# Attention scores split into high and low parts: two full passes and one shared pass for a pair of key tiles

## The chip, the core and the metric

The kernel runs on one core of a Trainium2 chip. The core has a matrix engine (TensorE, PE in the profile, with PEld for the loading of its weights), a vector engine (DVE), a scalar engine (ACT), GpSimd (POOL) and SyncE (SP); here SP does nothing but issue transfers, and POOL little else. The metric is the device time of one execution in microseconds (us). Before the change it is 1505.49 us, the median of 3 runs (1505.46 to 1505.99).

## The reference

Three stages follow each other; everything is float32.

```
scores = (1/S) * z @ z.T            # z: 2 x 3008 x 64, S = 3008
x      = u * (maximum(scores, 0)**2 @ v)      # u, v: 2 x 3008 x 256
h      = x @ moe_w_in                # 6016 x 256 by 256 x 2048
g      = (a0 + a1 h + a2 h^2 + a3 h^3) / (1 + |b0| |h| + |b1| h^2 + 1e-6)
y      = g @ moe_w_out               # back to 6016 x 256
h2     = y @ moe2_w_in;  g2 = max(h2, 0) + alpha * min(h2, 0)
out    = g2 @ moe2_w_out
```

Only the product z @ z.T is touched by the change.

## The kernel before

**Products in parts.** TensorE is fed with a rounded float32 (fp32r). So each operand is split into a high part (the rounded value) and a low part (what the rounding left), and a product is the sum of passes: high by high, high by low and low by high. A pass is one matmul of up to 512 columns with a weight load of 128 by 128 ahead of it. For the values of the attention and both dense stages a pass fills all 128 rows of the array. For the scores z has only 64 features, so high and low are stacked: a tile zA holds the high part of z in partitions 0 to 63 and the low part in 64 to 127 (`load_z`, L691 and L694), and a tile zB holds the same with the halves exchanged. With zA as weights, a pass over zA gives high by high plus low by low (L846), and a pass over zB gives the two mixed products (L847). zB is copied out of zA by two transfers of SP for each block of 512 queries (`a_begin`, L736); that of the first block is computed on ACT and DVE (L704, L707).

**Tiling.** The work of the attention goes by batch (2), block of 512 queries (6, the last with 448) and pair of key tiles (12 pairs of 2 times 128 keys). As scores are symmetric, only pairs on or right of the diagonal are computed. The others are the transposes of finished ones: DVE transposes a result (L772), SP writes it to memory (L787, "rt") and reads it back when it is due (L820, "rr"). A computed pair goes through `a_scores`: four matmuls (two key tiles, two passes each) into PSUM, relu with the scale on ACT (L853 or L861), the square (L866), and high and low for the next product (L449, L454). In the two last blocks of 448 queries the columns come in cuts of 256 and 192, so a computed pair is eight matmuls. `a_values` multiplies a pair with v: eight matmuls of L887 and four of L898.

**PSUM.** While no step of the first dense stage has begun, computed pairs take turns in several double tiles (two single tiles s, h, acc); after that all of them use the two single tiles s_78 and s_79.

**What sets the order.** Nothing is issued as it is written. Each operation is recorded in a `Plan` with a guessed duration, the buffers that it reads and writes, and the order of TensorE; a list scheduler (`Plan.order`) then runs the plan in guessed time and gives each other engine the ready operation that is due first. Constants such as PACE, SAME, SOONER, SAFE and DEBT steer it. While the attention runs, steps of the first dense stage ("m1", L1012 to L1029 on ACT and DVE) and the decoding of weights ("dec", L554 to L635) are let in whenever the vector work that is booked (`plan.debt`) is below DEBT; each matmul takes its guessed time off that debt. What has not got in by the end of the attention follows after it, among the steps of the two dense stages ("h" and "m" are their hidden tiles, "ghi" and "glo" the parts of the activations).

Of the kernel before, what the change touches and what calls it, by code (L numbers as in the profile page):

```python
# [14 lines left out]
PSUM = bass.MemoryType.PSUM  # L15
DRAM = bass.MemoryType.DRAM

PT, ZP, XP = 48, 8, 4

RING = 2048  # L20

CAREFUL = False

PACE = 25.0

SAME = 0.13

SOONER = 30.0

WIRE = 0.7  # L30

SAFE = 1.0

BACK = 3

PRE = 3

AFTER = 4.0

FIRST, NEXT = 6, 4  # L40

FILL, DEBT, EDGE = 0.97, 4.0, 4.0

LAG_A, LAG_M = 3, 2

HEAD, X1 = 38, 18

R0, RD = 2, 2.5

WARM = 13  # L50

KEEP = 2

BOUND = 122879.9921875

# [18 lines left out]
class Plan:  # L74
# [8 lines left out]
    def add(self, eng, dur, fn, r=(), w=(), level="att", after=0.0, horizon=None, data=0.0):  # L83
        o = Op()
        o.eng, o.dur, o.fn, o.level, o.after, o.data = eng, dur, fn, level, after, data
        o.horizon = horizon
        if eng == "PE":
            self.pe = o
            self.debt = max(self.debt - FILL * dur, 0.0)
        elif eng == "DVE":  # L90
            self.debt += dur
        o.pin = self.pe
        o.i = len(self.ops)
        o.next, o.need, o.allocs, o.takes, o.bufs = [], 0, [], [], []
        preds = {}

        def keys(x):
            if isinstance(x, tuple):
                return [(x[0], x[1])]
            return [(x, p) for p in range(x.parts)]  # L100

        seen = set()
        for group, writes in ((r, False), (w, True)):
            for x in group:
                b = x[0] if isinstance(x, tuple) else x
                if id(b) not in seen:
                    seen.add(id(b))
                    o.bufs.append(b)
                    b.users += 1
                    b.ops.append(o)  # L110
                for k in keys(x):
                    kk = (id(k[0]), k[1])
                    for p in self.wrote.get(kk, ()):
                        preds[p.i] = p
                    if writes:
                        for p in self.read.get(kk, ()):
                            preds[p.i] = p
                if writes and b.kind:
                    o.takes.append(b)
                    if not b.held:  # L120
                        b.held = True
                        o.allocs.append(b)
        for group, writes in ((r, False), (w, True)):
            for x in group:
                for k in keys(x):
                    kk = (id(k[0]), k[1])
                    if writes:
                        self.wrote[kk] = [o]
                        self.read[kk] = []
                    else:  # L130
                        self.read.setdefault(kk, []).append(o)
        for p in preds.values():
            p.next.append(o)
            o.need += 1
        self.ops.append(o)
        return o
# [54 lines left out]
    def order(self):  # L191
# [30 lines left out]
                queue[b.kind].append((o.late, o.i, o, b))  # L222
        head = dict.fromkeys(rooms, 0)
        for q in queue.values():
            q.sort()

        def fits(o, now):
            want = {}
# [81 lines left out]
def relu2_attention_rational_mlp_prelu_mlp(  # L310
# [56 lines left out]
    def big_room(nm):  # L367
        return room(nm, F32R, (P, 2, 2, 256))

    def z_room(nm):  # L370
        return Buf("z", lambda i: zp.tile([P, QB], F32R, tag=f"z{i}", name=nm))

    def x_room(nm):
        return Buf("x", lambda i: xp.tile([P, QB], F32R, tag=f"x{i}", name=nm), 1)
# [25 lines left out]
    def act(n, fn, r, w, psum=False, ptr=0, level="att", horizon=SOON):  # L400
        return plan.add("ACT", n / 1200 + (0.051 if psum else 0.094) + 0.094 * ptr, fn, r, w, level, horizon=horizon)

    def dve(n, fn, r, w, ptr=0, fast=False, level="att", horizon=SOON):
        return plan.add("DVE", n / (1920 if fast else 960) + 0.068 + 0.061 * ptr, fn, r, w, level, horizon=horizon)
# [252 lines left out]
        )  # L657
        store[jp] = t

    zA = {}  # L660

    zB = {}

    def q_side(z, b, j):

        t = z[b, j]().rearrange("p (s a r) -> p a s r", s=4, a=4)
        if qn[j] == QB:
            return [(0, QB, t)]
        return [(0, QB // 2, t[:, 0:2]), (QB // 2, qn[j], t[:, 2:4, 0:3])]

    def load_z(b, g):

        raw = room("zraw", F32, (P, 2 * QB))
        n = qn[g]
        sp(
            n / 2,
            lambda: nc.sync.dma_start(out=raw()[:, 0:n], in_=zt[b, :, g * QB : g * QB + n]),
            [],
            [raw],
        )  # L680
        m = n
        if n % P:
            sp(
                32,
                lambda: nc.sync.dma_start(out=raw()[:, n : n + HALF], in_=zt[b, :, S - HALF : S]),
                [],
                [raw],
            )
            m += HALF
        t = z_room("zA")  # L690
        dve(m, lambda: nc.vector.tensor_copy(t()[:, 0:m], raw()[:, 0:m]), [raw], [t], fast=True)  # L691
        dve(
            m,
            lambda: nc.vector.tensor_tensor(  # L694
                t()[HALF:P, 0:m], raw()[HALF:P, 0:m], t()[HALF:P, 0:m].bitcast(F32), ALU.subtract
            ),
            [raw, t],
            [t],
        )
        zA[b, g] = t  # L700
        if (b, g) == (0, 0):
            q = z_room("zB")
            zB[b, g] = q
            act(m, lambda: nc.scalar.copy(q()[HALF:P, 0:m], raw()[HALF:P, 0:m]), [raw], [q])  # L704
            dve(
                m,
                lambda: nc.vector.tensor_tensor(  # L707
                    q()[0:HALF, 0:m], raw()[0:HALF, 0:m], t()[0:HALF, 0:m].bitcast(F32), ALU.subtract
                ),
                [raw, t],  # L710
                [q],
            )

    blocks = [(b, j) for b in range(B) for j in range(NQ)]
# [11 lines left out]

    def a_begin(b, j):

        if (b, j) in zB:
            return  # L730
        n = qn[j]
        t, z = z_room("zB"), zA[b, j]
        for p0 in (0, HALF):
            sp(
                n / 4,
                lambda p0=p0: nc.sync.dma_start(  # L736
                    out=t()[p0 : p0 + HALF, :n].bitcast(F32),
                    in_=z()[HALF - p0 : P - p0, :n].bitcast(F32),
                ),
                [z],  # L740
                [(t, p0 // HALF)],
                horizon=SOONER,
            )
        zB[b, j] = t

    def folded(b, i, j):
        return i < j
# [65 lines left out]
    def a_scores(b, j, kp):  # L813
        n = qn[j]
        if folded(b, kp // 2, j):
            r, d = room("rr"), turned[b, kp // 2, j]
            s0 = kp % 2 * 2
            sp(
                n,
                lambda: nc.sync.dma_start(out=r()[:, :, :n], in_=d()[s0 : s0 + 2].rearrange("s p k -> p s k")),  # L820
                [d],
                [r],
            )
            ahl[b, j, kp] = hi_lo(r, n, kp)
            return
        r = room("r")

        pair = None
        if not opened:
            turn = kp % 3 if (b, j) == (0, 0) else direct[0] % 2  # L830
            direct[0] += 1
            if turn == 1:
                pair = h_room("sp")
            elif turn == 2:
                t2 = Buf("acc1", lambda i: at["acc1"][i])
                pair = t2
        for i in range(2):
            k = 2 * kp + i
            zk = zA[b, k // 4]
            s = (pair, i) if pair is not None else s_room("s")  # L840
            ks = slice((k % 4) * P, (k % 4 + 1) * P)

            def mm(s=s, i=i, zk=zk, ks=ks):
                o = pair()[:, i, :n] if pair is not None else s()[:, :n]
                for (c0, c1, x), (_, _, y) in zip(q_side(zA, b, j), q_side(zB, b, j)):
                    nc.tensor.matmul(o[:, c0:c1], zk()[:, ks], x, start=True, stop=False)  # L846
                    nc.tensor.matmul(o[:, c0:c1], zk()[:, ks], y, start=False, stop=True)  # L847

            pe(n, 2 if n == QB else 4, mm, [zk, zA[b, j], zB[b, j]], [s])
            if pair is None:  # L850
                act(
                    n,
                    lambda s=s, i=i: nc.scalar.activation(r()[:, i, :n], s()[:, :n], AF.Relu, scale=1.0 / S),  # L853
                    [s],
                    [(r, i)],
                    psum=True,
                )
        if pair is not None:
            act(
                2 * n,  # L860
                lambda: nc.scalar.activation(r()[:, :, :n], pair()[:, :, :n], AF.Relu, scale=1.0 / S),  # L861
                [pair],
                [r],
                psum=True,
            )
        act(2 * n, lambda: nc.scalar.activation(r()[:, :, :n], r()[:, :, :n], AF.Square), [r], [r])  # L866
        ahl[b, j, kp] = hi_lo(r, n, kp)
        if folded(b, j, kp // 2):
            turn_block(b, j, kp, r)
# [457 lines left out]
```

## Time and profile before

| | |
|---|---|
| median of 3 runs | 1505.49 us |
| profiled execution, its own time | 1505.41 us |
| its span | 1503.6 us |
| PE busy | 1493.3 us, 99% |
| DVE busy | 1408.5 us, 94% |
| ACT busy | 1193.4 us, 79% |
| POOL busy | 71.3 us, 5% |
| granted TensorE clock | 9 (full) in all 40 slices |

The profiled execution took 1.8 us more than its span, which runs from its first to its last recorded instruction. A record of a matmul or of a vector instruction reaches into that of the next one, since the engines work in a pipeline: the price of one in a dense row is the distance from its start to the next start, not its own length. Busy shares count the union of the records, and so make an engine look somewhat fuller than it is.

### The profile page before, as it was taken

Reading aid. Unit: us, or ns where it says so; the run is one execution under the profiler, and the core shown is the slowest. Engines: PE = TensorE matmul, PEld = TensorE weight load, DVE = VectorE, ACT = ScalarE, POOL = GpSimd, SP = SyncE. Lnnn points to the kernel's source line nnn. Section 1 sums busy time; section 2 is a strip of 40 time slices with the busy share of each in tenths; the row PEclk is TensorE's granted clock in tenths of the full one; section 3 lists DMA queues with packets and bytes.
Section 4 is the critical chain, followed back from the end, with each engine's and each line's share of the span. In section 5 each row is a group of like instructions: output and inputs, shape, how many; then the busy total and the mean of one; then the engine's idle time right before and its main releaser. Section 6 shows DMA issues by size and latency. Waiting matters only on the chain.

```text
span 1503.6 us, 17908 instructions
## 1 busy us (share of the span) xinstructions
PE 1493.3 (99%) x6677; PEld 1247.2 (83%) x6677; DVE 1408.5 (94%) x1449; ACT 1193.4 (79%) x1406; POOL 71.3 (5%) x98
## 2 busy tenths in 40 slices
PE   9999999999999999999999999999999999999999
PEld 7888888788788887888888888888888888888888
DVE  8998999989999999999999999999999999899963
ACT  8888877888987687778779778878777887788754
POOL 1000000101212110000000000000000000000000
PEclk9999999999999999999999999999999999999999
DMA  7987547576878773100000000000000000000000
GB/s 202 243 242 186 151 143 236 152 195 188 238 217 248 246 248 129 43 28 29 15 28 14 29 29 28 29 15 28 29 29 14 27 17 28 28 26 29 15 1 25
DMA packets 178887, 144.51 MB, mean 96 GB/s; under 512 B 132704, under 2 KB 147568, under 8 KB 178800
## 3 DMA queue, kind: packets, MB, share of 16 engines
q1 hardware_dynamic: 169168, 108.75, 25.8%
q0 software_dynamic: 9632, 34.62, 6.9%
q8 instruction: 52, 0.85, 0.2%
q14 instruction: 35, 0.29, 0.1%
HBM read 83.90 MB, written 56.62 MB: 93 GB/s over the span
## 4 chain that ended last, share of the span: by engine, by line
PE 90%; DVE 7%; issue 2%; DMA 1%; ACT 0%; SPq 0%; DVEq 0%; ACTq 0%
PE acc L887 35%; PE acc L898 17%; PE h L960 6%; PE h L959 6%; PE h L958 6%; PE m L959 5%; PE m L958 5%; PE m L960 5%; PE s L847 2%; PE s L846 2%; DVE alo L454 1%; PE acc L877 1%; DVE ghi L1026 1%; DVE t L1028 0%; DVE ab L1027 0%
## 5 line engine op out<-in xcount | busy, mean ns | idle before, releaser
L887 PE MATMUL acc<-ghi,w 128*128 128x512 f32 (+1 forms) x1472 | 360.7, 387 | 0.0
L887 PEld LDWEIGHTS acc<-ghi,w 128*128 128x128 f32 x1472 | 275.6, 188 | 54.9
L887 PE MATMUL acc<-ahi,vt 128*128 128x512 f32 (+1 forms) x1152 | 283.0, 387 | 2.4 <-DVE ut L931 1.5
L887 PEld LDWEIGHTS acc<-ahi,vt 128*128 128x128 f32 x1152 | 215.8, 188 | 46.8 <-DVE ut L931 1.9
L1014 ACT ACTIVATE t<-h,sc 128x1024 f32<-128x1024 f32 (+1 forms) x96 | 114.0, 1187 | 104.4 <-PE h L960 86.1
L898 PE MATMUL acc<-glo,w 128*128 128x512 f32 (+1 forms) x736 | 195.0, 387 | 0.0
L898 PEld LDWEIGHTS acc<-glo,w 128*128 128x128 f32 x736 | 137.8, 188 | 27.5
L960 PE MATMUL h<-xhi,w 128*128 128x512 f32 (+1 forms) x408 | 156.2, 383 | 0.0
L958 PE MATMUL h<-xhi,w 128*128 128x512 f32 (+1 forms) x408 | 156.1, 383 | 0.0
L959 PE MATMUL h<-xlo,w 128*128 128x512 f32 (+1 forms) x408 | 156.1, 383 | 0.0
L1081 ACT ACTIVATE m<-m,sc 128x512 f32<-128x512 f32 (+1 forms) x180 | 117.0, 693 | 43.8 <-PE m L960 41.0
L1017 DVE SCALAR_TENSOR_TENSOR ab<-sq,cb,ab 128x1024 f32<-128x1024 f32 (+1 forms) x96 | 120.7, 1258 | 29.3 <-ACT sq L1012 29.1
L898 PE MATMUL acc<-alo,vt 128*128 128x512 f32 (+1 forms) x552 | 146.6, 386 | 0.0
L958 PE MATMUL m<-xhi,w 128*128 128x512 f32 (+1 forms) x360 | 139.4, 387 | 1.6 <-DVE m L1087 1.4
L959 PE MATMUL m<-xlo,w 128*128 128x512 f32 (+1 forms) x360 | 139.3, 387 | 0.9 <-DVE xlo L454 0.9
L960 PE MATMUL m<-xhi,w 128*128 128x512 f32 (+1 forms) x360 | 139.2, 387 | 0.0
L1022 ACT ACTIVATE sq<-ab,one 128x1024 f32<-128x1024 f32 (+1 forms) x96 | 110.3, 1149 | 20.6 <-DVE t L1019 20.5
L454 DVE TENSOR_TENSOR glo<-m,ghi 128x1024 fp32r<-128x1024 f32 (+1 forms) x96 | 114.9, 1197 | 11.0 <-ACT ghi L449 11.0
L898 PEld LDWEIGHTS acc<-alo,vt 128*128 128x128 f32 x552 | 103.6, 188 | 20.3 <-DVE alo L454 0.2
L1026 DVE TENSOR_TENSOR ghi<-t,sq 128x1024 fp32r<-128x1024 f32 (+1 forms) x96 | 114.9, 1196 | 5.0 <-ACT sq L1023 4.0
L1087 DVE TENSOR_TENSOR m<-m 128x1024 f32<-128x1024 f32 (+1 forms) x90 | 108.5, 1205 | 10.1 <-ACT m L1081 10.1
L1029 DVE TENSOR_TENSOR glo<-t,sq 128x1024 fp32r<-128x1024 f32 (+1 forms) x96 | 114.9, 1197 | 2.0
(99 smaller groups left out, 2645.0 us busy)
## 6 DMA issues: line engine op xcount, KB each, us to landing
rt<-rt SPq DMA_DIRECT2D x220, 128.0 KB, 3.2
rr<-rt SPq DMA_DIRECT2D x40, 512.0 KB, 5.1
rr<-rt SPq DMA_DIRECT2D x20, 448.0 KB, 4.9
wraw<-in_moe_w_in_dram POOLq DMA_DIRECT2D x16, 512.0 KB, 5.4
wraw<-in_moe_w_out_dram POOLq DMA_DIRECT2D x16, 512.0 KB, 5.5
wd<-dec POOLq DMA_DIRECT2D x16, 512.0 KB, 5.0
w<-wd POOLq DMA_DIRECT2D x16, 512.0 KB, 6.2
x2d<-x SPq DMA_DIRECT2D x11, 512.0 KB, 2.6
```

The source lines that it names most:

```text
L454: lambda: nc.vector.tensor_tensor(lo(), src(), hi().bitcast(F32), ALU.subtract),
L887: nc.tensor.matmul(acc()[:, e, :n], w()[:, k, i, e * P : (e + 1) * P], hi()[:, i, :n], start=first and i == 0 and k == 0, stop=False,)
L898: nc.tensor.matmul(acc()[:, e, :n], w()[:, 0, i, e * P : (e + 1) * P], lo()[:, i, :n], start=False, stop=last and i == both - 1,)
L958: nc.tensor.matmul(acc, w_hi, hi, start=first, stop=False)
L959: nc.tensor.matmul(acc, w_hi, lo, start=False, stop=False)
L960: nc.tensor.matmul(acc, w_lo, hi, start=False, stop=last)
L1014: act(N, lambda: activation(c(t), c(h), AF.Identity, scale=a3, bias=a2), [h], [t], psum=True, ptr=2, **kw)
L1017: dve(N, lambda: stt(c(ab), c(sq), b1, c(ab), ALU.mult, ALU.add), [sq, ab], [ab], ptr=1, **kw)
L1022: act(N, lambda: activation(c(sq), c(ab), AF.Abs_reciprocal_sqrt, bias=one), [ab], [sq], ptr=1, **kw)
L1026: dve(N, lambda: tt(c(hi), c(t), c(sq), ALU.mult), [t, sq], [hi], **kw)
L1029: dve(N, lambda: tt(c(lo), c(t), c(sq), ALU.mult), [t, sq], [lo], **kw)
L1081: lambda i=i, f=f: nc.scalar.activation(t()[:, i, :n], h()[:, i, :n], AF.Copy, scale=al[:, f : f + 1]),
```

## The change

The tile zK replaces zA as weights. In it the halves alternate from key tile to key tile: in even key tiles partitions 0 to 63 hold the high part and 64 to 127 the low part, in odd key tiles the other way round. For the queries there are two tiles: zH with the high part in both halves, zL with the low part in both halves. One pass with zK as weights over zH gives high by high plus low by high (L859 of the changed kernel), one for each key tile. The missing high by low needs 64 rows only. For the even key tile these are the upper 64 partitions of zK, for the odd one the lower 64, so two matmuls of 64 rows in different halves of the array, into two PSUM tiles, do it for the pair (L856). The product of low by low is left out. Both small matmuls are booked in the plan as one operation of ROWS = 1.2 passes.

zH and zL of each further block are copied from zK by eight transfers of 64 partitions by two pieces of 128 columns (L745), where two transfers made zB before. Those of the first block are computed on DVE, and its zK on ACT. The first pair of all has its low matmuls last instead of first. There are 9 instead of 8 rooms for z tiles, and some of the planner's constants are other ones.

```diff
-PT, ZP, XP = 48, 8, 4
+PT, ZP, XP = 48, 9, 4
+ROWS = 1.2
-SOONER = 30.0
+SOONER = 45.0
...
     def load_z(b, g):
...
-        t = z_room("zA")
-        dve(m, lambda: nc.vector.tensor_copy(t()[:, 0:m], raw()[:, 0:m]), [raw], [t], fast=True)
-        dve(
-            m,
-            lambda: nc.vector.tensor_tensor(
-                t()[HALF:P, 0:m], raw()[HALF:P, 0:m], t()[HALF:P, 0:m].bitcast(F32), ALU.subtract
-            ),
-            [raw, t],
-            [t],
-        )
+        t = z_room("zK")
...
+            dve(m, lambda: nc.vector.tensor_copy(t()[:, 0:m], raw()[:, 0:m]), [raw], [t], fast=True)
+        for odd in range(2):
+            def low(odd=odd):
+                rows = slice(0, HALF) if odd else slice(HALF, P)
+                z = t()[rows].rearrange("p (c o k) -> p c o k", o=2, k=P)[:, :, odd]
+                r = raw()[rows, 0:m].rearrange("p (c o k) -> p c o k", o=2, k=P)[:, :, odd]
+                nc.vector.tensor_tensor(z, r, z.bitcast(F32), ALU.subtract)
+            dve(m // 2, low, [raw, t], [t])
...
     def a_begin(b, j):
...
-        for p0 in (0, HALF):
-            sp(
-                n / 4,
...
+        for store, nm in ((zH, "zH"), (zL, "zL")):
+            t = z_room(nm, 4)
+            for odd in range(2):
+                src = HALF * (odd ^ (nm == "zL"))
+                for p0 in (0, HALF):
...
+                        nc.sync.dma_start(out=cols[0][p0 : p0 + HALF], in_=cols[1][src : src + HALF])
+                    sp(64, move, [z], [(t, 2 * odd + p0 // HALF)], horizon=SOONER)
...
     def a_scores(b, j, kp):
...
-                for (c0, c1, x), (_, _, y) in zip(q_side(zA, b, j), q_side(zB, b, j)):
-                    nc.tensor.matmul(o[:, c0:c1], zk()[:, ks], x, start=True, stop=False)
-                    nc.tensor.matmul(o[:, c0:c1], zk()[:, ks], y, start=False, stop=True)
...
+        def lows(c0, c1, y):
+            for i in range(2):
+                rows = slice(HALF * i, HALF * i + HALF)
+                nc.tensor.matmul(at_i(i)[:, c0:c1], zk()[rows, keys_of(i)], y[rows], start=not late, stop=late)
+        def highs(i, c0, c1, x):
+            nc.tensor.matmul(at_i(i)[:, c0:c1], zk()[:, keys_of(i)], x, start=late, stop=not late)
...
+                pe(ROWS * z, 1, lambda: lows(c0, c1, y()), [zk, zL[b, j]], hs)
```

In the order of TensorE, a computed pair later in the attention reads thus; s_78 and s_79 are the PSUM tiles of the two key tiles, acc_81 the sum of the values. Before:

```order
L898 MATMUL acc_81<-alo,vt 128x512 x4
L846 MATMUL s_79<-zA 128x512
L847 MATMUL s_79<-zB,zA 128x512
L846 MATMUL s_78<-zA 128x512
L847 MATMUL s_78<-zB,zA 128x512
L887 MATMUL acc_81<-ahi,vt 128x512 x8
```

And now:

```order
L922 MATMUL acc_81<-alo,vt 128x512 x4
L856 MATMUL s_79<-zL,zK 128x512
L856 MATMUL s_78<-zL,zK 128x512
L859 MATMUL s_79<-zH,zK 128x512
L859 MATMUL s_78<-zH,zK 128x512
L911 MATMUL acc_81<-ahi,vt 128x512 x8
```

There are four matmul instructions still (6677 in all, as before), but the two of L856 have 64 rows each; both PSUM tiles are now written by the first two instructions, where the second tile was first touched by the third one.

On the queue of SP, at the change from the first to the second and third query block, before (rt and rr are the written and reread transposes, xd the result of a block):

```order
L820 DMA rr<-rt_0_1_99 128x2x512
L736 DMA zB<-zA 64x512 x2
L787 DMA rt_0_5_103<-rt 32x16x64 x6
L787 DMA rt_0_5_103<-rt 32x16x32 x2
L937 DMA xd_0_104<-ut 128x1024
```

And now:

```order
L946 DMA ut<-in_u_dram 128x2x512
L745 DMA zL<-zK 64x2x128
L791 DMA rt_0_5_103<-rt 32x16x64 x4
L745 DMA zH<-zK 64x2x128 x3
L791 DMA rt_0_5_103<-rt 32x16x64 x2
L791 DMA rt_0_5_103<-rt 32x16x32 x2
L745 DMA zH<-zK 64x2x128
L824 DMA rr<-rt_0_2_100 128x2x512
L745 DMA zL<-zK 64x2x128
L961 DMA xd_0_105<-ut 128x1024
```

The copies of z stand in ones and threes between the transfers of the transposes; on the whole queue they are 88 where they were 22.

On TensorE at the end of the attention, before (h_80 belongs to the first dense stage, m to the second; 18 steps of the first dense stage stand ahead of the last row of alo,vt in the whole program):

```order
L887 MATMUL acc_82<-ghi,w 128x512 x8
L898 MATMUL acc_82<-glo,w 128x512 x4
L887 MATMUL acc_81<-ahi,vt 128x448 x8
L898 MATMUL acc_81<-alo,vt 128x448 x4
L958 MATMUL m<-xhi,w 128x512
```

And now (14 steps of the first dense stage stand ahead of the last row of alo,vt):

```order
L922 MATMUL acc_81<-alo,vt 128x448 x4
L982 MATMUL h_80<-xhi,w 128x512
L983 MATMUL h_80<-xlo,w 128x512
L984 MATMUL h_80<-xhi,w 128x512
L911 MATMUL acc_82<-ghi,w 128x512 x8
L922 MATMUL acc_82<-glo,w 128x512 x4
L982 MATMUL m<-xhi,w 128x512
```

Four steps of the first dense stage have gone from the attention into what follows it. On DVE, 27 of the 32 decoded weights are begun by the last alo of the attention, where all 32 were, and 14 steps of the first dense stage instead of 17.

## Rows read from the trace of the kernel before

**Rows 1.** The page's busy times, and the granted clock in 40 slices
```profile
PE 1493.3 (99%) x6677; PEld 1247.2 (83%) x6677; DVE 1408.5 (94%) x1449; ACT 1193.4 (79%) x1406; POOL 71.3 (5%) x98
...
PEclk9999999999999999999999999999999999999999
```

**Rows 2.** The page's chain that ended last, by engine
```profile
PE 90%; DVE 7%; issue 2%; DMA 1%; ACT 0%; SPq 0%; DVEq 0%; ACTq 0%
```

**Rows 3.** Waits of PE: us in total, times, longest
```profile
PE acc L887 <- DVE ut L931: 1.5, 1, 1.5
...
PE s L847 <- DVE zB L707: 0.3, 1, 0.3
```

**Rows 4.** Timeline of PE, one computed pair: start us, length us
```profile
60.60 0.40 PE L846 MATMUL s<-zA 128*128 128x512 f32 x1
60.83 0.40 PE L847 MATMUL s<-zB,zA 128*128 128x512 f32 x1
...
61.53 0.39 PE L887 MATMUL acc<-ahi,vt 128*128 128x512 f32 x1
```

**Rows 5.** Timeline of PE, a pair in cuts of 256 and 192
```profile
226.76 0.28 PE L846 MATMUL s<-zA 128*128 128x256 f32 x1
...
227.66 0.64 PE L887 MATMUL acc<-ahi,vt 128*128 128x512 f32 x2
```

**Rows 6.** Groups of PE by form: count, busy us, mean ns
```profile
L846 PE MATMUL s<-zA 128*128 128x512 f32 x124 | 49.9, 402 | 0.1
...
L846 PE MATMUL h<-zA 128*128 128x512 f32 x28 | 11.5, 412 | 0.0
...
L846 PE MATMUL acc<-zA 128*128 128x512 f32 x8 | 3.6, 446 | 0.0
...
L846 PE MATMUL s<-zA 128*128 128x256 f32 x8 | 2.3, 292 | 0.0
```

**Rows 7.** Windows of attention and dense stages: busy of PE, PEld, DVE, ACT, POOL
```profile
0.00:572.00 572.00, 566.24 (x2504) 469.35 (x2505) 545.16 (x667) 471.40 (x590) 69.21 (x94) 1.00 0.74 211
...
600.00:1450.00 850.00, 849.03 (x3787) 707.88 (x3786) 817.72 (x740) 676.24 (x756) 0.53 (x1) 1.00 0.07 25
```

**Rows 8.** Groups of DVE: steps of the first dense stage, weights, z
```profile
L1017 DVE SCALAR_TENSOR_TENSOR ab<-sq,cb,ab 128x1024 f32<-128x1024 f32 x88 | 112.6, 1280 | 27.3 <-ACT sq L1012 27.1
L1019 DVE TENSOR_TENSOR t<-t,sq 128x1024 f32<-128x1024 f32 x88 | 107.3, 1219 | 0.0
...
L566 DVE SCALAR_TENSOR_TENSOR dec<-wraw,dec 128x512 int32<-128x512 int32 x32 | 22.0, 686 | 0.2
...
L694 DVE TENSOR_TENSOR zA<-zraw,zA 64x512 fp32r<-64x512 f32 x12 | 8.3, 690 | 0.4
...
L509 DVE TENSOR_TENSOR vt<-vt 64x256 fp32r<-64x256 f32 x2 | 0.8, 423 | 0.0
```

**Rows 9.** Timeline of DVE in the dense stages
```profile
904.69 1.22 DVE L454 TENSOR_TENSOR glo<-m,ghi 128x1024 fp32r<-128x1024 f32 x1
905.83 1.21 DVE L1019 TENSOR_TENSOR t<-t,sq 128x1024 f32<-128x1024 f32 x1
```

**Rows 10.** Tile zB: its issues on SP (ns min/median/max), and landing
```profile
L736 SPq DMA_DIRECT2D zB<-zA x22: 467/640/1929, 9.7 to 466.3; - x22
...
DMA to landing us min/median/max: 2.2/4.1/9.0
```

**Rows 11.** Timeline of DVE, then of PE, in the opening
```profile
3.83 0.69 DVE L694 TENSOR_TENSOR zA<-zraw,zA 64x512 fp32r<-64x512 f32 x1
4.55 0.43 DVE L691 CAST zA<-zraw 128x512 fp32r<-128x512 f32 x1
4.90 0.68 DVE L707 TENSOR_TENSOR zB<-zraw,zA 64x512 fp32r<-64x512 f32 x1
...
5.72 0.77 PE L847 MATMUL s<-zB,zA 128*128 128x512 f32 x1 [0.35 <-DVE zB L707]
```

**Rows 12.** Groups of ACT by form: the relu of one key tile
```profile
L853 ACT ACTIVATE r<-s 128x512 f32<-128x512 f32 x124 | 69.4, 605 | 28.2 <-PE s L847 25.5 <-PE acc L898 2.5
```

More of the change, by code (lines that the diff above doesn't have):

```diff
@@ L16 @@
 DRAM = bass.MemoryType.DRAM
-PT, ZP, XP = 48, 8, 4
+PT, ZP, XP = 48, 9, 4
+ROWS = 1.2
 RING = 2048
 CAREFUL = False
-PACE = 25.0
-SAME = 0.13
-SOONER = 30.0
+PACE = 28.0
+SAME = 0.16
+SOONER = 45.0
 WIRE = 0.7
-SAFE = 1.0
+SAFE = 0.5
 BACK = 3
 PRE = 3
[L38 to L44, printed above, removed]
+AFTER = 5.0
+FIRST, NEXT = 7, 2
+FILL, DEBT, EDGE = 0.97, 5.0, 5.0
+LAG_A, LAG_M = 4, 2
 HEAD, X1 = 38, 18
-R0, RD = 2, 2.5
+R0, RD = 3, 3
 WARM = 13
-KEEP = 2
+KEEP = 3
 BOUND = 122879.9921875
@@ L117, in add @@
                             preds[p.i] = p
-                if writes and b.kind:
+                if writes and b.kind and b not in o.takes:
                     o.takes.append(b)
@@ L224, in order @@
         for q in queue.values():
-            q.sort()
+            q.sort(key=lambda x: x[:2])
         def fits(o, now):
@@ L368, in big_room, with z_room @@
         return room(nm, F32R, (P, 2, 2, 256))
-    def z_room(nm):
-        return Buf("z", lambda i: zp.tile([P, QB], F32R, tag=f"z{i}", name=nm))
+    def z_room(nm, parts=2):
+        return Buf("z", lambda i: zp.tile([P, QB], F32R, tag=f"z{i}", name=nm), parts)
     def x_room(nm):
@@ L658, in fill_w, with part @@
         store[jp] = t
-    zA = {}
-    zB = {}
+    zK, zH, zL = {}, {}, {}
     def q_side(z, b, j):
[L666 to L669, printed above, removed]
+        def part(c0, c1):
+            t = z[b, j]().rearrange("p (s a r) -> p a s r", s=4, a=4)
+            return t if c1 - c0 == QB else t[:, 0:2] if c0 == 0 else t[:, 2:4, 0:3]
+        cuts = [(0, QB)] if qn[j] == QB else [(0, QB // 2), (QB // 2, qn[j])]
+        return [(c0, c1, lambda c0=c0, c1=c1: part(c0, c1)) for c0, c1 in cuts]
     def load_z(b, g):
@@ L689, in load_z @@
             m += HALF
-        t = z_room("zA")
-        dve(m, lambda: nc.vector.tensor_copy(t()[:, 0:m], raw()[:, 0:m]), [raw], [t], fast=True)
-        dve(
-            m,
-            lambda: nc.vector.tensor_tensor(
-                t()[HALF:P, 0:m], raw()[HALF:P, 0:m], t()[HALF:P, 0:m].bitcast(F32), ALU.subtract
-            ),
-            [raw, t],
-            [t],
-        )
[L700 to L704, printed above, removed]
-            dve(
-                m,
[L707 to L711, printed above, removed]
+        t = z_room("zK")
+        zK[b, g] = t
+        opening = (b, g) == (0, 0)
+        if opening:
+            act(m, lambda: nc.scalar.copy(t()[:, 0:m], raw()[:, 0:m]), [raw], [t])
+            x, y = z_room("zH"), z_room("zL")
+            zH[b, g], zL[b, g] = x, y
+            dve(m, lambda: nc.vector.tensor_copy(x()[:, 0:m], raw()[:, 0:m]), [raw], [x], fast=True)
+        else:
+            dve(m, lambda: nc.vector.tensor_copy(t()[:, 0:m], raw()[:, 0:m]), [raw], [t], fast=True)
[6 more added lines that the diff above has]
+            dve(m // 2, low, [raw, t], [t])
+        if opening:
+            dve(
+                m,
+                lambda: nc.vector.tensor_tensor(y()[:, 0:m], raw()[:, 0:m], x()[:, 0:m].bitcast(F32), ALU.subtract),
+                [raw, x],
+                [y],
             )
@@ L727, in a_begin, with move @@
     def a_begin(b, j):
-        if (b, j) in zB:
+        if (b, j) in zH:
             return
-        n = qn[j]
-        t, z = z_room("zB"), zA[b, j]
-        for p0 in (0, HALF):
-            sp(
-                n / 4,
[L736 to L744, printed above, removed]
+        z = zK[b, j]
+        for store, nm in ((zH, "zH"), (zL, "zL")):
[3 more added lines that the diff above has]
+                for p0 in (0, HALF):
+                    def move(t=t, odd=odd, src=src, p0=p0):
+                        cols = [x().bitcast(F32).rearrange("p (c o k) -> p c o k", o=2, k=P)[:, :, odd] for x in (t, z)]
+                        nc.sync.dma_start(out=cols[0][p0 : p0 + HALF], in_=cols[1][src : src + HALF])
+                    sp(64, move, [z], [(t, 2 * odd + p0 // HALF)], horizon=SOONER)
+            store[b, j] = t
     def folded(b, i, j):
@@ L836, in a_scores, with at_i, keys_of, low @@
                 pair = t2
[L837 to L844, printed above, removed]
-                for (c0, c1, x), (_, _, y) in zip(q_side(zA, b, j), q_side(zB, b, j)):
-                    nc.tensor.matmul(o[:, c0:c1], zk()[:, ks], x, start=True, stop=False)
-                    nc.tensor.matmul(o[:, c0:c1], zk()[:, ks], y, start=False, stop=True)
-            pe(n, 2 if n == QB else 4, mm, [zk, zA[b, j], zB[b, j]], [s])
-            if pair is None:
-                act(
-                    n,
-                    lambda s=s, i=i: nc.scalar.activation(r()[:, i, :n], s()[:, :n], AF.Relu, scale=1.0 / S),
-                    [s],
+        zk = zK[b, kp // 2]
+        hs = [(pair, i) if pair is not None else s_room("s") for i in range(2)]
+        def at_i(i):
+            return pair()[:, i, :n] if pair is not None else hs[i]()[:, :n]
+        def keys_of(i):
+            k = kp % 2 * 2 + i
+            return slice(k * P, (k + 1) * P)
+        late = (b, j, kp) == (0, 0, 0)
+        def lows(c0, c1, y):
[4 more added lines that the diff above has]
+            nc.tensor.matmul(at_i(i)[:, c0:c1], zk()[:, keys_of(i)], x, start=late, stop=not late)
+        for (c0, c1, x), (_, _, y) in zip(q_side(zH, b, j), q_side(zL, b, j)):
+            z = c1 - c0
+            def low(c0=c0, c1=c1, y=y):
+                pe(ROWS * z, 1, lambda: lows(c0, c1, y()), [zk, zL[b, j]], hs)
+            if not late:
+                low()
+            for i in range(2):
+                pe(z, 1, lambda i=i, c0=c0, c1=c1, x=x: highs(i, c0, c1, x()), [zk, zH[b, j]], [hs[i]])
+            if late:
+                low()
+        if pair is None:
+            for i in range(2):
+                act(
+                    n,
+                    lambda i=i: nc.scalar.activation(r()[:, i, :n], hs[i]()[:, :n], AF.Relu, scale=1.0 / S),
+                    [hs[i]],
                     [(r, i)],
```

## The prediction

> **What bounds the kernel now.** I read the page's busy times first [rows 1]: TensorE is busy for 1493.3 of 1503.6 us, and the granted clock is at its full level in every slice, so nothing is to be had from the clock. A busy share alone does not say that an engine sets the end, so next come the chain of waits, which runs over PE for 90% of the span [rows 2], and the waits of PE itself [rows 3]: six in all, the longest 1.5 us, the shortest 0.3, some 6 us together. The reader is to see that TensorE hardly ever waits for anybody: a cycle taken out of its stream comes off the end, as long as the others keep up. DVE is the one that could fail to: 94% over the span, and 817.7 of 850 us in the dense stages [rows 1, 7].
>
> **The price of a pass.** The recorded length of a matmul (0.40) is not its price, as the records overlap. In a computed pair the four matmuls and the next one start at 60.60, 60.83, ... 61.53 [rows 4]: 0.93 us for four, 0.2325 each. 512 columns at 2.4 GHz take 0.2133, so 0.0192 is fixed per matmul, the new weights included. The cut pairs agree: eight matmuls of 256 and 192 columns take 0.90 us (226.76 to 227.66, [rows 5]), so one of each take 0.225, of which 448 columns are 0.187, and again 0.019 is left for each.
>
> **How many pairs.** L846 ran 124, 28 and 8 times with 512 columns into s, h and acc [rows 6]: 160, one for each key tile, so 80 full pairs. With 256 columns it ran 8 times: 4 pairs in cuts.
>
> **The passes removed.** A full pair took four passes. Now it takes two, 0.465 us, and the shared one. No instruction of the trace uses half of the array's rows, so its price has to be bounded. Lower end: the two matmuls run side by side and cost one pass, 0.2325; under that it cannot go, since 512 columns are still streamed, and the full clock leaves no faster rate. Upper ends: if they run one after the other they cost two passes, 0.465, and nothing is won. If, besides, or instead, the array has to run empty each time that the number of rows changes, that costs at most what a recorded matmul still has to go when its successor starts, 0.40 - 0.2325 = 0.163 [rows 4] (unrounded: 0.395), twice in a pair. I take side by side, with two fixed parts, 0.2133 + 2 x 0.0192 = 0.252, and 0.02 for each of the two changes, 0.292 in all. The reason for the 0.02: the row nearest to such a change is the change of weights ahead of every matmul, which costs no more than the fixed part of 0.019; the 0.163 is a latency that consecutive matmuls hide in every row of this trace. That the halves do run at the same time is the choice on which the forecast stands; for it speaks that they use other rows, other weights and other PSUM tiles, and that weight loads are no obstacle: a matmul of 192 columns with its own full weight load fits into about 0.1 us [rows 5], so two loads fit behind one pass.
>
> So a full pair goes from 0.930 to 0.465 + 0.292 = 0.757, and 80 of them save 80 x 0.173 = 13.8 us. A cut pair: from 0.90 to 0.450 for the four full matmuls, 0.187 + 4 x 0.019 = 0.263 for the shared ones and four changes, 0.08; that is 0.794, and 4 x 0.106 saves 0.4 us. Together 14.3.
>
> The Trainium skill, on the page "TensorE: Matmul & The Clock Gate", Part 3, puts the span of matmuls packed into different row groups at one matmul and about 4 ns for each further one. By that a pair would save 0.2325 - 0.004 = 0.228, and the sum would be 18 to 19 us; no run here shows it yet.
>
> **What is added.** On DVE: the preparation of a z tile was a copy and one subtraction over 64 partitions of 512, 690 ns; now it is the copy and two over 256 columns each, for which the nearest row is 423 ns [rows 8]. 12 tiles make 12 x (2 x 423 - 690) = 1.9 us. It lies in the attention, where DVE is idle for 572 - 545 = 27 us [rows 7], and PE does not wait for it, but for the first tile. Without that cover it would cost 1.9.
>
> The opening: before, DVE did the cast, L694, the next tile's cast and L707, and the second matmul started at 5.72 [rows 11]. Now DVE has a cast, a subtraction of the full tile, one of half the columns, the next tile's cast and again one of half, before the second key tile can begin; with the starts of [rows 11] (0.72, 0.35 and 0.70 us apart) that is about 0.45 + 0.7 + 0.4 + 0.35 + 0.4 after 3.4, so 5.7 again. I book nothing, within 0.5 either way.
>
> On SP: 88 issues instead of 22, at 0.64 us [rows 10], 42 us more of its time in 572. Behind them stand the transposes' writes and reads and the u tiles; who waits for those is ACT and DVE, and then the values on PE. The copies land in 2.2 to 9.0 us [rows 10] and may now be issued up to 45 us ahead in the plan's time. I book nothing; at worst each of the 11 block changes shows a late copy as the longest landing less the median, 5 us, but PE waited for none of the copies before [rows 3].
>
> The two single PSUM tiles: the low matmuls of a pair need both, so the second must be free 0.465 - 0.25 = 0.2 us sooner. Between two computed pairs stand at least twelve matmuls of values, some 2.7 us at about 0.23 each, and the two relus take 2 x 0.605 [rows 12]. Nothing booked.
>
> **What is moved.** With cheaper pairs less is taken off the booked vector debt, and four steps of the first dense stage and five weights go past the end of the attention (three of the steps on DVE). For PE that is the same work later. For DVE it is 3 x (1.28 + 6 x 1.22) = 26 us and at most 5 x 8 x 0.69 = 27 us more after the attention [rows 8], while PE's part there grows by 4 x 24 x 0.23 = 22 us. DVE was idle for 850 - 817.7 = 32 us there [rows 7]; 32 + 22 - 53 leaves 1 us by records. But a record of 1.22 is followed 1.14 later by the next [rows 9], so 7% of the busy time, some 55 us, is overlap, and the true room is far larger. No stall booked; the first place to look for one is the beginning of the dense stages.
>
> **The sum.** 1505.41 (the profiled execution's own time, 0.08 under the median) - 14.3 = 1491.1, so 1491 for the median too. The likeliest case has a range of its own of 1486 (a pass for nothing, 80 x 0.2325 + 4 x 0.225 = 19.5 saved) to 1498 (changes three times as dear, 0.06 each: 80 x 0.08 = 6.4 less, and a us of new waits).
>
> **Rivals.** (1) The array runs empty at each change of the number of rows. Then a pair takes 0.465 + 0.252 + 2 x 0.163 = 1.043, 0.113 more than before; 80 x 0.113 = 9.0, and the cut pairs, with four changes each, 4 x (0.450 + 0.263 + 0.652 - 0.90) = 1.9: 1516. It gets slower than before from 0.107 us for each change. The Trainium skill, "TensorEngine Tiling (Array Packing)", Tiling Modes, Key Properties, says that changing the tiling mode drains TensorE, though different tiles work in parallel; it gives no price. For it: a computed pair stands alone among full matmuls, so each pays both changes. Against it: in the trace no change of weights, width or PSUM tile opens a gap. Chance 0.14. (2) The halves run one after the other, the change doing nothing for the time: 1505, with small changes of 0.02 at most 1509. For it: nothing in the trace shows two matmuls at work at once. Chance 0.12. (3) Side by side, but half of the gain goes to changes of 0.06 to 0.08 or to waits for copies, reads or vector work at the denser places: 1498 to 1502. Against it: the idle times above. Chance 0.11. The forecast keeps 0.63.
>
> **Chances and range.** A measurement of this kernel tells some 0.2% from no change, 3 us. Faster by more: the forecast and (3), 0.74. Slower by more: (1), and a small part of (2), 0.15. Within: 0.11. The range of 1486 to 1508 holds the forecast, (3), and (2) nearly whole, and leaves out most of (1).
>
> **What would show it.** In the profile after: the two matmuls of L856 start within some 0.05 us of each other and the next one of L859 about 0.25 to 0.3 later (right); 0.23 between the two (serial); a gap of 0.1 or more ahead of L856 and again ahead of L859 (running empty). A computed pair takes about 0.76 from its first start to the first L911. PE still waits for under 10 us in all, DVE is at 95%. The prediction is wrong if a pair takes 0.9 or more, or if PE's waits grow beyond 10 us.

## The result and the profile after

The changed kernel takes 1520.12 us (median of 4 runs, 1519.92 to 1521.21), the kernel before beside it 1505.63 (4 runs); the ratio is 1.0097, 95% interval 1.008 to 1.0115. It is 14.5 us slower, where 14.3 us faster was forecast.

The page's busy times and the granted clock of the changed kernel, the counterpart of [rows 1]:

```profile
PE 1509.4 (99%) x6677; PEld 1226.4 (81%) x6677; DVE 1411.8 (93%) x1461; ACT 1188.2 (78%) x1406; POOL 74.3 (5%) x98
...
PEclk9999999999999999999999999999999999999999
```

DVE has 3 us more to do, ACT 5 less; PE is busy 16 us longer with the same number of matmuls at the same clock. So the time is in TensorE's own stream, and the waits of PE (us in total, times, longest) confirm it; there are four, 4.9 us together, against 6.4 for the kernel before [rows 3]:

```profile
PE acc L911 <- DVE ut L955: 1.6, 2, 1.4
PE s L443 <- DVE one L425: 1.4, 1, 1.4
PE m L982 <- DVE m L1111: 1.2, 1, 1.2
PE s L859 <- DVE zK L708: 0.7, 1, 0.7
```

The timeline of PE around one computed pair (start us, length us, line, tile, shape, number), the counterpart of [rows 4], shows where it sits:

```profile
61.92 0.39 PE L922 MATMUL acc<-alo,vt 128*128 128x512 f32 x1
62.24 0.51 PE L856 MATMUL s<-zL,zK 64*128 64x512 f32 x2
62.68 0.74 PE L859 MATMUL s<-zH,zK 128*128 128x512 f32 x2
63.25 0.39 PE L911 MATMUL acc<-ahi,vt 128*128 128x512 f32 x1
```

The two matmuls of 64 rows (64*128) together fill 0.51 us where one alone has a record of 0.50 (run e2 below): they do run side by side. But they start 0.32 after the last matmul of the values, where 0.23 is the usual distance; the first of L859 comes 0.44 after them; and the pair of L859 needs 0.57 to the next matmul instead of 2 x 0.2325 = 0.465. From the point at which a full pass could have started, 61.92 + 0.23 = 62.15, to 63.25 the pair takes 1.10 us. Before it took 0.93, and 0.757 was forecast.

The loading of weights shows what stands ahead of each of them. Timeline of PEld, the changed kernel, the same place:

```profile
61.47 0.41 PEld L922 LDWEIGHTS acc<-alo,vt 128*128 128x128 f32 x2
62.24 0.18 PEld L856 LDWEIGHTS s<-zL,zK 64*128 64x128 f32 x2 [0.35 <-issue]
62.68 0.30 PEld L859 LDWEIGHTS s<-zH,zK 128*128 128x128 f32 x2 [0.25 <-issue]
63.02 0.42 PEld L911 LDWEIGHTS acc<-ahi,vt 128*128 128x128 f32 x2
```

And the kernel before, at the pair of [rows 4]:

```profile
60.38 0.19 PEld L846 LDWEIGHTS s<-zA 128*128 128x128 f32 x1
60.60 0.19 PEld L847 LDWEIGHTS s<-zB,zA 128*128 128x128 f32 x1
60.84 0.19 PEld L846 LDWEIGHTS s<-zA 128*128 128x128 f32 x1
```

Before, the weights of a matmul are loaded while its predecessor runs: the load for the matmul of 60.83 starts at 60.60, with the matmul of 60.60. After, the loader stands idle for 0.35 and 0.25 us at each change between 128 and 64 rows, and load and matmul have one and the same start, 62.24 and 62.68: the load lies in the open.

A pair in cuts changes its number of rows four times (counterpart of [rows 5], PE):

```profile
228.89 0.39 PE L856 MATMUL s<-zL,zK 64*128 64x256 f32 x2
229.21 0.50 PE L859 MATMUL s<-zH,zK 128*128 128x256 f32 x2
229.64 0.36 PE L856 MATMUL s<-zL,zK 64*128 64x192 f32 x2
229.93 0.47 PE L859 MATMUL s<-zH,zK 128*128 128x192 f32 x2
230.23 2.03 PE L911 MATMUL acc<-ahi,vt 128*128 128x512 f32 x8
```

With the 0.09 ahead of its first matmul it takes 1.43 us instead of 0.90. The bill: 80 x (1.10 - 0.93) + 4 x (1.43 - 0.90) = 15.7 us, less 1.5 us of waits that are gone: 14.2, of 14.5 measured.

The windows that answer to [rows 7] (busy of PE, PEld, DVE, ACT, POOL) show the moved work: less DVE in the attention, more behind it, and no stall from that.

```profile
0.00:572.00 572.00, 568.14 (x2442) 436.56 (x2443) 518.14 (x642) 450.63 (x566) 66.12 (x86) 1.00 0.75 208
...
600.00:1450.00 850.00, 850.00 (x3788) 708.81 (x3787) 835.14 (x757) 687.93 (x772) 1.07 (x2) 1.00 0.08 26
```

### The profile page after: what moved, and what is told of

The parts are those of the page before. It is cut to its first block, busy times and chain, and to the rows that moved or that the text cites. A ratio compares the mean times of both kernels' runs of the same rounds, so it can differ in the third digit from the quotient of the medians.

```text
span 1518.1 us, 18085 instructions
## 1 busy us (share of the span) xinstructions
PE 1509.4 (99%) x6677; PEld 1226.4 (81%) x6677; DVE 1411.8 (93%) x1461; ACT 1188.2 (78%) x1406; POOL 74.3 (5%) x98
## 4 chain that ended last, share of the span: by engine, by line
PE 98%; DVE 1%; ACT 1%; DMA 0%; issue 0%; DVEq 0%; ACTq 0%
PE acc L911 39%; PE acc L922 19%; PE h L984 6%; PE h L983 6%; PE h L982 6%; PE m L982 5%; PE m L984 5%; PE m L983 5%; PE s L859 3%; PE s L856 2%; PE acc L901 1%; PE h L859 1%; PE h L856 0%; DVE m L1111 0%; DVE ut L955 0%; PE acc L859 0%
## 5 line engine op out<-in xcount | busy, mean ns | idle before, releaser
L982 PE MATMUL h<-xhi,w 128*128 128x512 f32 (+1 forms) x412 | 157.9, 383 | 0.0
L984 PE MATMUL h<-xhi,w 128*128 128x512 f32 (+1 forms) x412 | 157.9, 383 | 0.0
L1041 DVE SCALAR_TENSOR_TENSOR ab<-sq,cb,ab 128x1024 f32<-128x1024 f32 (+1 forms) x96 | 121.1, 1261 | 19.5 <-ACT sq L1036 19.2
L1105 ACT ACTIVATE m<-m,sc 128x512 f32<-128x512 f32 (+1 forms) x178 | 112.8, 694 | 18.1 <-PE m L984 18.1
L1052 DVE TENSOR_TENSOR t<-t,ab 128x1024 f32<-128x1024 f32 (+1 forms) x96 | 115.0, 1198 | 0.3
```

The costliest lines, as they stand in the source:

```text
L982: nc.tensor.matmul(acc, w_hi, hi, start=first, stop=False)
L984: nc.tensor.matmul(acc, w_lo, hi, start=False, stop=last)
L1041: dve(N, lambda: stt(c(ab), c(sq), b1, c(ab), ALU.mult, ALU.add), [sq, ab], [ab], ptr=1, **kw)
L1052: dve(N, lambda: tt(c(t), c(t), c(ab), ALU.subtract), [t, ab], [t], **kw)
L1105: lambda i=i, f=f: nc.scalar.activation(t()[:, i, :n], h()[:, i, :n], AF.Copy, scale=al[:, f : f + 1]),
```

## The experiments

Theory, formed from these rows: each change of the number of rows costs about 0.20 us, and nothing else in the change matters; (1.10 - 0.465 - 0.2325) / 2 = 0.20. Rivals: the half-row matmuls are slow themselves (a price per matmul), or the loss comes from the copies of z, the planner's numbers and the moved steps. Unless it says otherwise, a kernel is the changed one with its planned costs, and so nearly its order, kept.

**e1, all 128 rows for the low matmuls.**

```diff
-                rows = slice(HALF * i, HALF * i + HALF)
+                rows = slice(0, P)
```

> The changed kernel with its order kept, but the low matmuls take all 128 rows (zL in both halves, so low by low is added): four full passes for a pair, no change of the number of rows. If the loss comes from the half-row matmuls (whatever the reason), the 0.17 us of each of 84 pairs goes: 1504 to 1507 us. If it comes from the other copies of z, the planner's numbers or the moved steps, it stays: 1517 to 1521 us.

Measured: 1505.53 us, ratio to before 0.9998 (0.9988 to 1.0007). The whole loss goes with the half-row matmuls; the other copies, the new constants, and the four steps and five weights that moved cost nothing that can be told. PE at a pair of e1:

```profile
62.76 0.63 PE L856 MATMUL h<-zL,zK 128*128 128x512 f32 x2
63.23 0.63 PE L859 MATMUL h<-zH,zK 128*128 128x512 f32 x2
63.69 2.01 PE L911 MATMUL acc<-ahi,vt 128*128 128x512 f32 x8
```

Four passes in 0.93 us, as before.

**e2, one low matmul instead of two.**

```diff
-            for i in range(2):
+            for i in range(1):
...
-            nc.tensor.matmul(at_i(i)[:, c0:c1], zk()[:, keys_of(i)], x, start=late, stop=not late)
+            nc.tensor.matmul(at_i(i)[:, c0:c1], zk()[:, keys_of(i)], x, start=late or i == 1, stop=not late or i == 1)
```

> Leaves out the low matmul of the odd key tile; one half-row matmul stands where two stood, between the same two changes of the number of rows. Price per change (the array runs empty and the next weights are loaded in the open): the two had run side by side, so taking one away saves next to nothing: 1517 to 1520 us. Price per half-row matmul (they run one after the other, or each is slow): half of 0.635 us goes in each of 84 pairs, 1520 - 27 = 1493 us.

Measured: 1520.43 us, ratio 1.0096 (1.0081 to 1.0111). The second half-row matmul is free. PE:

```profile
63.48 0.50 PE L856 MATMUL s<-zL,zK 64*128 64x512 f32 x1
63.91 0.74 PE L859 MATMUL s<-zH,zK 128*128 128x512 f32 x2
64.48 2.00 PE L911 MATMUL acc<-ahi,vt 128*128 128x512 f32 x8
```

One matmul holds the place for 0.43 us, two held it for 0.44.

**e4, the low matmuls twice.**

```diff
-            for i in range(2):
+            for again in (False,) if late else (False, True):
+                for i in range(2):
...
+                    first = not (late or again)
...
```

> Issues the two low matmuls of a pair twice in a row (adds high by low a second time): four half-row matmuls between the same two changes. Price per change: one more pass of 0.2325 to 0.25 us side by side, 84 x 0.24 = 20 us, 1540 us. Price per half-row matmul: 84 x 0.635 = 53 us more, 1573 us.

Measured: 1540.43 us, ratio 1.023 (1.0213 to 1.0247); 20.3 us above the changed kernel. PE:

```profile
63.71 0.74 PE L858 MATMUL s<-zL,zK 64*128 64x512 f32 x4
64.38 0.73 PE L861 MATMUL s<-zH,zK 128*128 128x512 f32 x2
64.95 2.00 PE L913 MATMUL acc<-ahi,vt 128*128 128x512 f32 x8
```

Four in 0.67 us, two in 0.44: a further round of two costs 0.23, as much as a full pass. As long as the number of rows stays the same, half-row matmuls side by side are as good as hoped for, weight loads included.

**e5, four changes instead of two.** The low matmul of each key tile is put ahead of the high one of the same tile; `lows` is left empty.

```diff
...
-        def highs(i, c0, c1, x):
+        def highs(i, c0, c1, x, y):
+            rows = slice(HALF * i, HALF * i + HALF)
+            for low in (not late, late):
+                if low:
+                    nc.tensor.matmul(at_i(i)[:, c0:c1], zk()[rows, keys_of(i)], y[rows], start=not late, stop=late)
+                else:
+                    nc.tensor.matmul(at_i(i)[:, c0:c1], zk()[:, keys_of(i)], x, start=late, stop=not late)
...
```

> The two low matmuls of a pair are put apart (low, high, low, high), so a pair has four changes of the number of rows instead of two and the lows no longer run side by side; the output is the same. Price per change, 0.20 us as read from the changed kernel: 2 x 0.20 + 0.2325 more for each of 84 pairs, 53 us: 1573 us. Price per pair, whatever the number of changes in it: only the second pass comes in, 84 x 0.2325 = 20 us: 1540 us.

Measured: 1575.13 us, ratio 1.0462 (1.0444 to 1.0479). The price is one per change. PE:

```profile
65.71 0.50 PE L860 MATMUL s<-zL,zK 64*128 64x512 f32 x1
66.14 0.50 PE L862 MATMUL s<-zH,zK 128*128 128x512 f32 x1
66.57 0.50 PE L860 MATMUL s<-zL,zK 64*128 64x512 f32 x1
67.00 0.50 PE L862 MATMUL s<-zH,zK 128*128 128x512 f32 x1
67.34 0.85 PE L914 MATMUL acc<-ahi,vt 128*128 128x512 f32 x3
```

Each matmul between two changes takes 0.43 to the next start, whether it has 64 or 128 rows, 0.20 more than a pass. The last one, which follows a change but has none behind it, takes 0.34: of the 0.20 some 0.11 lies behind a change, where the load is in the open, and 0.09 ahead of one, where the next load has not begun.

**e9, the low matmuls of two pairs together.** Early in the attention, where a pair has PSUM tiles of its own, two pairs are recorded as low, low, high, high.

```diff
+                    first = a_scores(b, j, kp)
+                    next(first, None)
...
+                        second = a_scores(b, j, direct_kps[0])
+                        next(second, None)
...
+                    for _ in first:
+                        pass
```

(`a_scores` stops with a yield behind its low matmuls; only the core of the diff is shown.)

> Early in the attention, where a pair finds PSUM tiles of its own, the low matmuls of two pairs stand together ahead of the high ones of both: 144 changes of the number of rows in the program instead of 174, the same matmuls. Price per change of 0.20 us: 30 x 0.20 = 6 us less than the changed kernel, 1514 us. Price per low matmul: no change, 1520 us.

Measured: 1513.57 us, ratio 1.0052 (1.0037 to 1.0067); 6.5 us under the changed kernel, as 30 changes fewer ask for. PE at such a group:

```profile
68.69 0.51 PE L856 MATMUL s<-zL,zK 64*128 64x512 f32 x2
69.04 0.40 PE L856 MATMUL h<-zL,zK 64*128 64x512 f32 x2
69.37 0.74 PE L859 MATMUL s<-zH,zK 128*128 128x512 f32 x2
69.94 0.63 PE L859 MATMUL h<-zH,zK 128*128 128x512 f32 x2
70.41 1.78 PE L914 MATMUL acc<-ahi,vt 128*128 128x512 f32 x7
```

Two pairs take 1.72 + 0.09 = 1.81 us, two times 0.905. That is under the 0.93 of four full passes, but by so little that the 30 pairs which can be grouped would win less than 1 us if all the others kept four full passes; no run shows that mix. Larger groups need more PSUM tiles than the kernel has while it works on the first dense stage.

These rows also part the 0.20. The first two low matmuls have a change ahead of them only and take 0.35 to the next start, 0.12 over a pass. The second two have one behind them only and take 0.33, 0.10 over a pass. The high ones take 0.57 behind the change, 0.105 over two passes, and 0.47 away from it. So both directions cost alike, some 0.09 to 0.10 ahead of the change and 0.11 behind it.

**e3, no low matmuls.**

```diff
-            for i in range(2):
-                rows = slice(HALF * i, HALF * i + HALF)
-                nc.tensor.matmul(at_i(i)[:, c0:c1], zk()[rows, keys_of(i)], y[rows], start=not late, stop=late)
+            pass
...
-            nc.tensor.matmul(at_i(i)[:, c0:c1], zk()[:, keys_of(i)], x, start=late, stop=not late)
+            nc.tensor.matmul(at_i(i)[:, c0:c1], zk()[:, keys_of(i)], x, start=True, stop=True)
```

> Leaves out the product of high by low: two full passes a pair, nothing else. Both theories: all that the shared pass costs goes, 84 x 0.635 = 53 us, so 1467 us, unless another engine becomes the bound on the way (then up to 1480).

Measured: 1492.07 us, ratio 0.9908 (0.9893 to 0.9923). A miss: 25 us more than the sum of passes asks for. The waits of PE, the three largest of ten:

```profile
PE acc L909 <- DVE ut L953: 6.0, 3, 2.4
PE s L857 <- ACT r L875: 3.0, 3, 2.7
PE acc L920 <- DVE alo L456: 2.5, 3, 1.2
```

The ten add up to 20.5 us, and 16 of them lie beyond what the changed kernel waits. Up to 5 us more went to the clock: around three waits of 2.2 to 2.7 us the granted clock is 0.86, 0.79 and 0.83 of full speed (from 124 to 136 us, 260 to 268 and 313 to 323). So a second point of the forecast was open: would a pass that is really free come off the end? The next three runs take away one pass of four, without any half-row matmul.

**e10, three full passes.**

```diff
-            for i in range(2):
-                rows = slice(HALF * i, HALF * i + HALF)
+            for i in range(1):
+                rows = slice(0, P)
...
-            nc.tensor.matmul(at_i(i)[:, c0:c1], zk()[:, keys_of(i)], x, start=late, stop=not late)
+            nc.tensor.matmul(at_i(i)[:, c0:c1], zk()[:, keys_of(i)], x, start=late or i == 1, stop=not late or i == 1)
```

> Leaves out the low matmul of the odd key tile and gives the even one all 128 rows: three full passes a pair, in the changed kernel's order. It is what the change would be if a change of the number of rows cost nothing. If TensorE stays the bound: 1505.5 - 84 x 0.2325 = 1486 us. If the others take over as soon as two passes are gone (the run without low matmuls stopped at 1492 instead of 1467): 1492 us or more.

Measured: 1495.4 us, ratio 0.9931 (0.9916 to 0.9946): 10 us come off, half of the 19.5. The largest waits of PE:

```profile
PE acc L911 <- DVE ut L955: 3.4, 3, 1.4
PE s L856 <- ACT r L877: 2.1, 4, 1.1
PE m L982 <- DVE m L1111: 2.0, 2, 1.2
```

All its waits make 11.8 us, against 4.9 of the changed kernel and 6.4 of the kernel before. The time lies in the range of the second expectation, 1492 us or more, but its reason holds in part only: TensorE stays the bound for most of the attention and loses to DVE and ACT at single places. Nine us are missing. e1, with four full passes in the same order, waits 6.2 us, so 5.6 of the nine are added waits; the rest is not accounted for.

**e12, the same, booked at its cost.** e10 with ROWS = 1.0 in the plan.

```diff
-ROWS = 1.2
+ROWS = 1.0
```

> As the run with three full passes (it leaves out the low matmul of the odd key tile), but booked in the plan at what it costs, ROWS = 1.0 instead of 1.2, so the list scheduler makes a new order. If the 9 us that were missing there (1495 instead of 1486) went because the order was made for a dearer pair: 1486 to 1490 us. If ACT and DVE are too full in the attention for any such order: 1493 to 1497 us.

Measured: 1507.72 us, ratio 1.0013 (1.0004 to 1.0022); both expectations missed. With the same matmuls as e10, and the better estimate in the plan, the new order is 12 us slower. The largest of its waits of PE:

```profile
PE acc L911 <- DVE ut L955: 5.4, 4, 2.7
PE acc L911 <- ACT ahi L451: 3.1, 3, 2.1
PE m L982 <- DVE m L1111: 2.8, 1, 2.8
```

All its waits make 20.6 us, 8.8 more than in e10, and around two of them the granted clock falls, where e10 keeps it at 1.00 from 0 to 600 us. Two windows of e12 (busy of PE, PEld, DVE, ACT, POOL, then the granted clock):

```profile
262.00:276.00 14.00, 11.35 (x44) 8.96 (x43) 9.19 (x12) 11.60 (x16) 0.00 (x0) 0.88 0.27 71
566.00:580.00 14.00, 11.07 (x42) 8.47 (x41) 13.88 (x18) 8.32 (x11) 2.72 (x6) 0.88 0.69 225
```

They lack 0.12 of 14 us each, up to 3.4 us of work together, so waits and clock cover the 12 us. The order alone moves the time by more than half of the pass that was to be saved. Why the scheduler's new order brings these waits is not settled.

**e13, the kernel before with three passes.**

```diff
-                    nc.tensor.matmul(o[:, c0:c1], zk()[:, ks], x, start=True, stop=False)
-                    nc.tensor.matmul(o[:, c0:c1], zk()[:, ks], y, start=False, stop=True)
+                    nc.tensor.matmul(o[:, c0:c1], zk()[:, ks], x, start=True, stop=i == 1)
+                    if i == 0:
+                        nc.tensor.matmul(o[:, c0:c1], zk()[:, ks], y, start=False, stop=True)
```

> The kernel before with one of its four passes of each pair left out (the mixed products of the odd key tile), in its own order. If TensorE stays the bound, 1505.5 - 84 x 0.2325 = 1486 us. If the other engines of the attention give way, as in the changed kernel's order, about 1495 us; then the limit is in the kernel and not in the copies of z or the new order.

Measured: 1501.35 us, ratio 0.9968 (0.9957 to 0.9979): 4.5 us of 19.5, less than either expectation. Its timeline of PE shows the worst place:

```profile
269.87 3.78 PE L888 MATMUL acc<-ahi,vt 128*128 128x512 f32 x8 [3.25 <-DVE ut L932]
273.45 1.91 PE L899 MATMUL acc<-alo,vt 128*128 128x512 f32 x4
...
276.16 2.01 PE L888 MATMUL acc<-ahi,vt 128*128 128x512 f32 x8
```

PE waits 3.25 us for the vector engine at the end of a block, and the eight matmuls behind it take 3.78 us where the same eight take 2.01 at 276.16. All its waits make 16.6 us, 10.2 more than in the kernel before. The cover is thin in the old order too, so the limit is in the kernel and not in the copies of z or the new order.

## Why the prediction was wrong

- **What bounds the kernel** was right for the kernel as it stands: the loss is in TensorE's stream, and PE waits no longer than before (4.9 us against 6.4). Only "at its full level in every slice" is too much: in the opening the matmuls start 0.43 apart (8.42 and 8.84 in the kernel before), which is the distance at the lower level, though the clock row shows 9.
- **Side by side** was right. One half-row matmul or two take the same time (e2), and a further round of two costs 0.23 us (e4).
- **The price of a change failed**: "I take side by side, with two fixed parts, ... and 0.02 for each of the two changes". It is 0.20 (e5: 0.43 - 0.23; e9: 6.5 us for 30 changes, 0.22 each). A shared pass so costs 0.635 us instead of 0.292, and 84 pairs turn from 14.3 us won into 14.5 lost. I took the price from the row that looked nearest, the change of weights between two full matmuls. But that row is cheap only because the load is hidden behind the predecessor, and the hiding is what a change of rows takes away, as the PEld rows show.
- **The upper bound** of 0.163 was too low for the same reason: it counted the tail of the predecessor, of which 0.09 to 0.10 showed, and not the load of the successor, 0.11. That is why rival (1), the nearest to the right one by its mechanism, came to 1516 instead of 1520. The range ended short of the result because it left this rival out, at a chance of 0.14. The sentence of the Trainium skill that spoke for it ("TensorEngine Tiling (Array Packing)", Tiling Modes, Key Properties: changing the tiling mode drains TensorE) agrees with the trace, where a change costs 0.20.
- **The other price of a pair**: the Trainium skill, "TensorE: Matmul & The Clock Gate", Part 3, has about 4 ns for a further matmul in other rows. For the group by itself e2 agrees (0.44 us for two, 0.43 for one). The estimate of 18 to 19 us worked out from that figure did not come true, as each group here pays for two changes.
- **"A cycle taken out of its stream comes off the end, as long as the others keep up"** would have failed too. A pass taken away for nothing gives 10 us of 19.5 (e10), 4.5 (e13) or nothing (e12), depending on the order. Even with changes that cost nothing, the changed kernel's order would thus have come to some 1495 us and not to 1491. Six short waits in the trace of before say that the others keep up at the pace of that trace; they do not say by how much. I compared sums of DVE's idle time over hundreds of us, but PE waits for the last link of a chain at single places, such as the end of a block (ut).
- **Added and moved work** at nothing was right in sum: e1 has the new copies, the new preparation, the new constants and the new opening, and takes 1505.53. Term by term it is not shown. After its first 36 matmuls of values e1 stands at 24.49 us with eight computed pairs done, the kernel before at 22.33 us with seven. With 0.93 for the eighth, e1 is some 1.2 us behind there, more than the 0.5 that was allowed for the opening, and still it does not end later.

The split of the 0.20 into 0.11 behind a change and 0.09 to 0.10 ahead of it is read from the distances in e5 and e9. That the first part is the load in the open and the second the array running empty is read from the PEld rows; no run takes away one of the two alone.

## What to carry to other kernels

Matmuls of 64 rows side by side would have had to stand in longer rows of their own to pay here: going into them and out of them cost 0.40 us together, against 0.23 for the pass of 512 columns that they save, and grouping two pairs only just broke even. When a price is taken from a neighbouring row, ask what hides it there, and whether the change keeps that cover. And before counting a removed instruction of a busy engine in full, take it away in a run: the scheduler's order decided between 10 us and nothing.

## What the runs showed of the hardware that I had not expected

- A change between 128 and 64 rows costs 0.20 us at the full clock, in either direction (e5: 0.43 from start to start for both kinds, where a full pass among its like takes 0.23; e9 for each direction). In the changed kernel the next weight load does not start before the matmul ahead has nearly ended: at 62.24 and 62.68 load and matmul start together.
- The clock fell in the course of the wait of 3.25 us in e13. Two windows there, with PE idle and around its return (busy of PE, PEld, DVE, ACT, POOL, then the granted clock):

```profile
266.60:268.70 2.10, 0.02 (x1) 0.00 (x0) 2.04 (x3) 2.10 (x5) 0.00 (x0) 1.00 0.73 291
268.00:276.00 8.00, 6.13 (x15) 4.83 (x16) 7.85 (x12) 3.98 (x6) 2.20 (x2) 0.57 0.35 109
```

From 269.87 to 273.45 eight matmuls are 0.45 apart, so TensorE runs at its lower level of 1.2 GHz, and at 276.16 it is back at 2.4. Twelve matmuls at half speed cost some 12 x 0.22 = 2.6 us on top of the wait, so this stall of PE cost nearly twice its own length. Another wait of 2.5 us in the same run (for ahi, up to 386.54) left the clock at full.
